# Lightning attention and a gated MLP on one core: all casts on POOL, weights requested behind them, states ahead of scores

## The chip, the cores and the metric

The kernel runs on one core of one Trainium2 chip. Its time is the device time of one execution in microseconds, the median of several runs. Five engines run their own instruction streams and wait for one another through semaphores: PE (matmul), DVE (vector), ACT (activation), POOL (GpSimd) and SP, which here only issues DMAs. ACT and POOL issue DMAs too.

## What is computed

A linear attention with decay works in blocks of 64 tokens with a running state for each head; its output, laid out as tokens by 512 channels, goes through an MLP whose gate mixes tokens. Cut to what matters:

```python
batch, n_heads, seq, head_dim = (4, 8, 768, 64)       # d_model 512, d_ff 1024
for b in range(nb):                                    # blocks of 64 tokens
    intra = einsum('bhic,bhjc->bhij', qb, kb) * Dmask  # lam ** (i - j), i >= j
    intra = einsum('bhij,bhjd->bhid', intra, vb)
    inter = einsum('bhid,bhde->bhie', qb * lam_pow, kv_state)
    out[:, :, sl] = intra + inter
    kv_state = lam_block * kv_state + einsum('bhsd,bhse->bhde', kb * rev_pow, vb)

x = out.transpose(0, 2, 1, 3).reshape(B, S, H * D)
h = maximum(x @ w_in, 0)
u, v = h[..., :512], h[..., 512:]
v_n = (v - mean(v)) / sqrt(var(v) + 1e-6)              # over channels
v_s = einsum('ts,bsd->btd', w_spatial, v_n) + b_spatial[None, :, None]
return (u * v_s) @ w_out
```

Inputs and output are float32; the kernel works in bfloat16 with sums in float32.

## The kernel before

The kernel takes blocks of 128 tokens instead of 64, which is the same recurrence. A *step* is 256 tokens of one batch with all heads: three steps a batch, twelve in all. For each step n there are these groups, whose short names are used from here on:

- lk:n, `load_step`, five DMAs from SP: k in two halves, q, v in two halves, 1.5 MB together, into four buffers each (`fin`);
- c:n, `cast_step`: kd (k times decay), qc and vc, the bfloat16 copies. kd is DVE's in the first three steps and POOL's behind them; qc is ACT's, vc POOL's;
- T:n, `trans_step`: 16 transposes of kd and qc on PE, evicted by ACT (kT) and DVE (qT);
- A:n, `scores_step`: 16 matmuls, masked by DVE (a);
- K:n, `kv_step`: the state's update, PE and then DVE (sd, s);
- O:n, `out_step`: the states of this step and the one before times q, and a times v; ACT evicts it as xT.

For each batch b the MLP follows: pv:b:r (the half of W_in that is normalised, one for each step r; ACT's relu, then DVE's statistics, ACT's root, DVE's normalised rows vn), pu:b:r (the other half, evicted as uT), pvs:b:f (four groups of products with w_spatial and the bias, multiplied by u on DVE into gT) and po:b:r (w_out, evicted by ACT, written by an output DMA from SP). wt:s are the transposes of w_spatial, done once in three pieces and evicted by ACT as wt_sb; pvs needs all three.

Weights come through POOL's DMA queue, which casts them to bfloat16: win:1 (the half for pv, 512 KB in the core), win:0 (the half for pu), wsp (w_spatial, 1152 KB, with the bias), wout (512 KB).

The orders of PE and POOL are written out by hand (`manual_schedule`); those of DVE, ACT and SP are made by a scheduler. On PE a loop over steps puts A:n+1, O:n, K:n+1 and T:n+2, and fills in pieces of the MLP from a list `pend`. On POOL win:1 is requested first, win:0 behind the cast of step 0, wsp and wout behind that of step 1.

Of the kernel before, what the change touches and what calls it, by code (L numbers as in the profile page):

```python
# [18 lines left out]
def kernel(  # L19
# [12 lines left out]
    nc = tc.nc  # L32
    P = 128
    B, H, S, D = q.shape
    DM = H * D
    DFF = moe_w_in.shape[1]
    DH = DFF // 2
    NBLK = S // P
    NG = H // 2
    NCH = DM // P  # L40
# [16 lines left out]
        return psum.tile(shape, dt, tag="ps", name=name)  # L57


    lam_bc = const.tile([P, H], FP32)  # L60
    nc.scalar.dma_start(out=lam_bc, in_=lam.unsqueeze(0).to_broadcast((P, H)))

    st = {}

    def load_step(n):
        b, r = divmod(n, NR)
        toks = slice(r * T2, (r + 1) * T2)
        q_in = fin.tile([P, H, 2, D], FP32, tag="q_in", name=f"q_in_{n}")
        k_in = fin.tile([P, H, 2, D], FP32, tag="k_in", name=f"k_in_{n}")
        v_in = fin.tile([P, H, 2, D], FP32, tag="v_in", name=f"v_in_{n}")  # L70
# [22 lines left out]

    qpos = iota_f([P, 2, 2, D], [[1, 2], [0, 2], [2, D]], 1, 0, "qpos")

    rel = iota_f([P, 2, D], [[1, 2], [2, D]], 0, -1, "rel")

    win_sb = wpool.tile([P, NCH, DFF], BF16)
    wout_sb = wpool.tile([P, NCH, DM], BF16)
    bsp_bc = wpool.tile([P, S], BF16)  # L100
    wt_sb = wpool.tile([P, NBLK, S], BF16)
    wsp_raw = wpool.tile([P, NBLK, S], BF16)

    def load_win(f0, f1):
        nc.gpsimd.dma_start(out=win_sb[:, :, f0:f1],
                            in_=moe_w_in.rearrange("(g p) f -> p g f", p=P)[:, :, f0:f1])

    load_win(DH, DFF)
    for n in range(1, 4):
        load_step(n)  # L110


    loglam = const.tile([P, H], FP32)
    nc.scalar.activation(out=loglam, in_=lam_bc, func=AF.Ln)
# [15 lines left out]
    nc.vector.tensor_scalar(out=causal, in0=rel.rearrange("p m d -> p (m d)"), scalar1=0.0,  # L130
                            scalar2=None, op0=ALU.is_ge)
    amask = const.tile([P, 2, 2, 2, P], FP32)
    for h in range(H):
        nc.vector.tensor_scalar(out=amask[:, h // 4, h % 2, (h // 2) % 2, :], in0=causal,
                                scalar1=lm128[:, h:h + 1], scalar2=None, op0=ALU.mult)
    eps_t = const.tile([P, 1], FP32)
    nc.vector.memset(eps_t, 1e-6)
    oo128 = const.tile([P, P], BF16)
    nc.vector.memset(oo128, 1.0 / P)


    xT = {}

    def cast_step(n):
        s = st[n]
        kd = att.tile([P, 2, H, D], BF16, tag="kd", name=f"kd_{n}")
        qc = att.tile([P, 2, H, D], BF16, tag="qc", name=f"qc_{n}")
        vc = att.tile([P, H, 2, D], BF16, tag="vc", name=f"vc_{n}")
        eng = nc.vector if n < NR else nc.gpsimd
        eng.tensor_tensor(out=kd.rearrange("p c h d -> p h c d"), in0=s["k_in"],  # L150
                          in1=ldec.unsqueeze(2).unsqueeze(3).broadcast_to((P, H, 2, D)),
                          op=ALU.mult)
        nc.scalar.activation(out=qc.rearrange("p m h d -> p h m d"), in_=s["q_in"], func=AF.Copy)  # L153
        nc.gpsimd.tensor_copy(out=vc, in_=s["v_in"])  # L154
        s["kd"], s["qc"], s["vc"] = kd, qc, vc

# [112 lines left out]
    def pv(b, r):  # L269
        if r == 0:  # L270
            gmlp_tiles(b)
        x, m = xT[b], gm[b]
        vh, mv, rstd = m["vh"], m["mv"], m["rstd"]
        ps = two_banks([P, 2, DH], f"pv_{b}_{r}")
        for j in range(2):
            for c in range(NCH):
                nc.tensor.matmul(out=ps[:, j], lhsT=x[:, r, c, j * P:(j + 1) * P],  # L277
                                 rhs=win_sb[:, c, DH:DFF], start=(c == 0), stop=(c == NCH - 1))
        pair = slice(2 * r, 2 * r + 2)
        nc.scalar.activation(out=vh[:, pair, :], in_=ps, func=AF.Relu)  # L280
        for t in (2 * r, 2 * r + 1):
# [54 lines left out]
        nc.scalar.activation(out=wt_sb[:, s:s + 2, :], in_=ps[:, :, 0:S], func=AF.Copy)  # L336


    pend = []

    def fill(n):
        for _ in range(min(n, len(pend))):
            pend.pop(0)()

    def after_out(n):
        b, r = divmod(n, NR)
        pend.append(lambda: pv(b, r))
        if r == 0:
            pend.append(lambda: pu(b, 0))
        if r == NR - 1:  # L350
            pend.append(lambda: pu(b, 1))
            pend.append(lambda: pu(b, 2))
            if b == 0:
                pend.extend([lambda s=s: wt_piece(s) for s in (0, 2, 4)])
            pend.extend([lambda f=f: pvs(b, f) for f in range(NCH)])
            pend.extend([lambda i=i: po(b, i) for i in range(NR)])

    with tc.manual_schedule(engines={PE, mybir.EngineType.Pool}):
        cast_step(0)
        load_win(0, DH)  # L360
        cast_step(1)
        nc.gpsimd.dma_start(out=wsp_raw, in_=moe_w_spatial.rearrange("(a p) s -> p a s", p=P))
        nc.gpsimd.dma_start(out=bsp_bc, in_=moe_b_spatial.unsqueeze(0).to_broadcast((P, S)))
        nc.gpsimd.dma_start(out=wout_sb, in_=moe_w_out.rearrange("(t p) f -> p t f", p=P))
        trans_step(0)
        scores_step(0)
        kv_step(0)
        trans_step(1)
        load_step(4)
        fills = {0: 1, 1: 2, 2: 5}  # L370
        for n in range(NS):
            if n + 2 < NS:
                cast_step(n + 2)
            if n + 5 < NS:
                load_step(n + 5)
            if n + 1 < NS:
                scores_step(n + 1)
            out_step(n)
            after_out(n)
            if n + 1 < NS:  # L380
                kv_step(n + 1)
            f = fills.get(n, 4 + (n % 3 == 0))
            fill(f // 2)
            if n + 2 < NS:
                trans_step(n + 2)
            fill(f - f // 2)
        fill(len(pend))


# [28 lines left out]
```

## Time and profile before

| | us |
|---|---|
| median of 3 runs | 187.28 (186.24 to 187.67) |
| the profiled execution | 188.46 |
| its span | 186.7 |
| PE busy in it | 145.7 (78%) |
| DVE, ACT, POOL busy | 103.4, 89.1, 34.8 |
| HBM read, written | 24.78 MB, 6.29 MB |

A profile row with a start says: start, duration, engine, line, operation, output and inputs, shapes, count, and in brackets how long the engine idled before and what ended that. Rows of grouped instructions give the total, then the mean of one in ns. A windows row gives a stretch, its length, and the busy time of each engine with its number of instructions; then the granted PE clock (1.00 is full), the share of the DMA engines and what they moved in GB/s. PE's busy time is partly modelled. Times within the span are what the text reckons with; the time of an execution is 1.76 us longer than its span here.

### The profile page before, as it was taken

Reading aid. Unit: us, or ns where it says so; the run is one execution under the profiler, and the core shown is the slowest. Engines: PE = TensorE matmul, PEld = TensorE weight load, DVE = VectorE, ACT = ScalarE, POOL = GpSimd, SP = SyncE. Lnnn points to the kernel's source line nnn. Section 1 sums busy time; section 2 is a strip of 40 time slices with the busy share of each in tenths; the row PEclk is TensorE's granted clock in tenths of the full one; section 3 lists DMA queues with packets and bytes.
Section 4 is the critical chain, followed back from the end, with each engine's and each line's share of the span. In section 5 each row is a group of like instructions: output and inputs, shape, how many; then the busy total and the mean of one; then the engine's idle time right before and its main releaser. Section 6 shows DMA issues by size and latency. Waiting matters only on the chain.

```text
span 186.7 us, 3638 instructions
## 1 busy us (share of the span) xinstructions
PE 145.7 (78%) x1540; PEld 96.5 (52%) x1540; DVE 103.4 (55%) x191; ACT 89.1 (48%) x98; POOL 34.8 (19%) x35
## 2 busy tenths in 40 slices
PE   0005677507979779999997999999799999999980
PEld 0005563305649556655776665575676646565430
DVE  1029993705399853542989747169884722564400
ACT  4244324712677942268775613666722157660051
POOL 4004060006245344060606005020000000000000
PEclk9999996975999979999999999999999999999999
DMA  4999969999999999999998900530000027000035
GB/s 98 218 211 252 205 161 184 199 212 232 199 241 248 200 239 238 221 225 222 330 254 195 252 8 0 208 133 4 0 0 4 2 79 262 0 0 4 0 132 205
DMA packets 68337, 28.36 MB, mean 152 GB/s; under 512 B 50528, under 2 KB 65248, under 8 KB 68320
## 3 DMA queue, kind: packets, MB, share of 16 engines
q1 hardware_dynamic: 65664, 25.17, 56.5%
q0 software_dynamic: 2512, 2.95, 9.6%
q8 instruction: 12, 0.20, 0.5%
q14 instruction: 5, 0.04, 0.1%
q10 hardware_dynamic: 144, 0.00, 0.0%
HBM read 24.78 MB, written 6.29 MB: 166 GB/s over the span
## 4 chain that ended last, share of the span: by engine, by line
PE 54%; SPq 13%; DVE 11%; ACT 9%; DMA 9%; issue 2%; POOL 1%; ACTq 0%; POOLq 0%
PE pvs L307 17%; PE po L322 11%; DMA v_in<-in_v_dram 9%; PE pv L277 8%; PE pu L297 7%; SPq L77 6%; SPq L72 5%; PE pt L163 4%; DVE a L192 3%; PE pvs L309 3%; SPq L74 3%; DVE st L282 3%; ACT vh L280 2%; ACT wt_sb L336 2%; DVE vn L288 2%
## 5 line engine op out<-in xcount | busy, mean ns | idle before, releaser
L307 PE MATMUL pvs<-wt_sb,vn 128*128 128x384 bf16 x192 | 37.8, 331 | 2.1 <-ACT wt_sb L336 2.0
L192 DVE TENSOR_TENSOR a<-pam,amask 128x1024 bf16<-128x1024 f32 x24 | 28.5, 1210 | 6.0 <-PE pam L189 6.0
L154 POOL CAST vc<-v_in 128x1024 bf16<-128x1024 f32 x12 | 12.9, 1074 | 84.0 <-DMA v_in<-in_v_dram 42.7
L252 ACT ACTIVATE xT<-pat 128x1024 bf16<-128x1024 f32 x12 | 15.8, 1320 | 23.7 <-PE pat L249 23.6
L307 PEld LDWEIGHTS <-vn 128*128 128x128 bf16 x192 | 18.9, 99 | 14.9 <-issue 2.5
L297 PE MATMUL pu<-xT,win_sb 128*128 128x256 bf16 x192 | 24.4, 285 | 1.9 <-DVE a L192 1.9
L311 DVE TENSOR_TENSOR gT<-pvs,uT 128x768 bf16<-128x768 f32 x16 | 15.3, 958 | 18.2 <-PE pvs L309 18.1
L277 PE MATMUL pv<-win_sb,xT 128*128 128x512 bf16 x96 | 24.2, 400 | 1.2 <-ACT xT L252 1.2
L322 PE MATMUL po<-wout_sb,gT 128*128 128x512 bf16 x96 | 21.9, 379 | 1.5 <-DVE a L192 1.1
L297 PEld LDWEIGHTS <-win_sb 128*128 128x128 bf16 x192 | 19.2, 102 | 5.7 <-issue 1.8
L153 ACT ACTIVATE qc<-q_in 128x1024 bf16<-128x1024 f32 x12 | 12.7, 1055 | 19.0 <-DMA q_in<-in_q_dram 19.0
L325 ACT ACTIVATE o<-po 128x1024 f32<-128x1024 f32 x12 | 12.3, 1025 | 19.0 <-PE po L322 19.0
L282 DVE BATCH_NORM_STATS2 st<-vh 128x6 f32<-128x512 bf16 x24 | 15.6, 682 | 10.4 <-ACT vh L280 10.3
L163 PE MATMUL pt<-ident,kd 128*128 128x128 bf16 x96 | 8.6, 242 | 15.5 <-DVE kd L150 15.5
L170 DVE TENSOR_TENSOR qT<-pt,lq 128x1024 bf16<-128x1024 bf16 x12 | 8.2, 684 | 18.5 <-ACT kT L168 18.5
L150 POOL TENSOR_TENSOR kd<-k_in,ldec 128x1024 bf16<-128x1024 f32 x9 | 17.1, 1897 | 6.1 <-DMA k_in<-in_k_dram 6.1
L168 ACT ACTIVATE kT<-pt 128x1024 bf16<-128x1024 bf16 x12 | 12.2, 1021 | 11.2 <-PE pt L163 11.2
L280 ACT ACTIVATE vh<-pv 128x1024 bf16<-128x1024 f32 x12 | 12.3, 1024 | 8.8 <-PE pv L277 8.8
L163 PEld LDWEIGHTS <-kd 128*128 128x128 bf16 x96 | 7.2, 110 | 17.4 <-DVE kd L150 15.7
L277 PEld LDWEIGHTS <-xT 128*128 128x128 bf16 x96 | 9.5, 102 | 11.7 <-issue 1.7
L322 PEld LDWEIGHTS <-gT 128*128 128x128 bf16 x96 | 9.2, 98 | 11.9 <-issue 1.0
L299 ACT ACTIVATE uT<-pu 128x1024 bf16<-128x1024 f32 x12 | 12.2, 1020 | 5.9 <-PE pu L297 5.8
(52 smaller groups left out, 146.2 us busy)
## 6 DMA issues: line engine op xcount, KB each, us to landing
k_in<-in_k_dram SPq DMA_DIRECT2D x24, 256.0 KB, 5.8
q_in<-in_q_dram SPq DMA_DIRECT2D x12, 512.0 KB, 6.1
v_in<-in_v_dram SPq DMA_DIRECT2D x24, 256.0 KB, 6.0
out_dram<-o SPq DMA_DIRECT2D x12, 512.0 KB, 3.4
wsp_raw<-in_moe_w_spatial_dram POOLq DMA_DIRECT2D x1, 1152.0 KB, 11.3
win_sb<-in_moe_w_in_dram POOLq DMA_DIRECT2D x2, 512.0 KB, 8.4
wout_sb<-in_moe_w_out_dram POOLq DMA_DIRECT2D x1, 512.0 KB, 14.8
bsp_bc<-in_moe_b_spatial_dram POOLq DMA_DIRECT2D x1, 192.0 KB, 11.7
```

The costliest lines, as they stand in the source:

```text
L150: eng.tensor_tensor(out=kd.rearrange("p c h d -> p h c d"), in0=s["k_in"], in1=ldec.unsqueeze(2).unsqueeze(3).broadcast_to((P, H, 2, D)), ...
L154: nc.gpsimd.tensor_copy(out=vc, in_=s["v_in"])
L163: nc.tensor.transpose(out=pt[:, j, g, c * P:(c + 1) * P], in_=src[:, c, 2 * g:2 * g + 2, :].rearrange("p h d -> p (h d)"), identity=ident)
L192: nc.vector.tensor_tensor(out=a_sb[:, i].rearrange("p h g c x -> p (h g) c x"), in0=pam.rearrange("p h g c x -> p (h g) c x"), in1=amask[: ...
L252: nc.scalar.activation(out=xT[b][:, r].rearrange("p g (c d m) -> p (g c) m d", c=2, m=2), in_=po.rearrange("p g c (m d) -> p (g c) m d", m ...
L277: nc.tensor.matmul(out=ps[:, j], lhsT=x[:, r, c, j * P:(j + 1) * P], rhs=win_sb[:, c, DH:DFF], start=(c == 0), stop=(c == NCH - 1))
L280: nc.scalar.activation(out=vh[:, pair, :], in_=ps, func=AF.Relu)
L282: nc.vector.bn_stats(out=m["st6"][:, t, :], in_=vh[:, t, :])
L297: nc.tensor.matmul(out=ps[:, f], lhsT=win_sb[:, c, f * P:(f + 1) * P], rhs=x[:, r, c, :], start=(c == 0), stop=(c == NCH - 1))
L307: nc.tensor.matmul(out=ps[:, i, 0:HW_], lhsT=m["vn"][:, s, f * P:(f + 1) * P], rhs=wt_sb[:, s, cols], start=(s == 0), stop=False)
L311: nc.vector.tensor_tensor(out=m["gT"][:, f, :].rearrange("p (i x) -> p i x", i=2), in0=ps[:, :, 0:HW_], in1=m["uT"][:, f, :].rearrange("p ...
L322: nc.tensor.matmul(out=ps[:, j], lhsT=gT[:, c, t * P:(t + 1) * P], rhs=wout_sb[:, c, :], start=(c == 0), stop=(c == NCH - 1))
```

## The change

All twelve casts of q and k join those of v on POOL, with four buffers each instead of three. The weights are requested behind casts: win:1 behind that of step 0, win:0, wsp and wout behind that of step 2. In the first steps K comes ahead of A. T, A, K and O of step 3 come behind the first two pvs of batch 0; before, T and A of steps 3 and 4 stood ahead of them. SP's order is now written by hand too, and the constants are formed a little earlier. Everything up to step 5 is a list of words, the rest a loop with a rule for each position in a batch.

```diff
+    ctx.enter_context(tc.manual_schedule(engines={PE, mybir.EngineType.Pool,
+                                                  mybir.EngineType.SP}))
+    for n in range(4):
+        load_step(n)
...
-    load_win(DH, DFF)
-    for n in range(1, 4):
-        load_step(n)
...
+    sq_t = const.tile([P, 1], FP32)
+    nc.scalar.activation(out=sq_t, in_=eps_t, func=AF.Sqrt)
...
+    def load_wsp():
+        nc.gpsimd.dma_start(out=wsp_raw, in_=moe_w_spatial.rearrange("(a p) s -> p a s", p=P))
+        nc.gpsimd.dma_start(out=bsp_bc, in_=moe_b_spatial.unsqueeze(0).to_broadcast((P, S)))
...
     def cast_step(n):
         s = st[n]
-        kd = att.tile([P, 2, H, D], BF16, tag="kd", name=f"kd_{n}")
...
-        eng = nc.vector if n < NR else nc.gpsimd
-        eng.tensor_tensor(out=kd.rearrange("p c h d -> p h c d"), in0=s["k_in"],
...
-        nc.scalar.activation(out=qc.rearrange("p m h d -> p h m d"), in_=s["q_in"], func=AF.Copy)
+        kd = att.tile([P, 2, H, D], BF16, tag="kd", bufs=4, name=f"kd_{n}")
...
+        nc.gpsimd.tensor_tensor(out=kd.rearrange("p c h d -> p h c d"), in0=s["k_in"],
...
+        nc.gpsimd.tensor_copy(out=qc.rearrange("p m h d -> p h m d"), in_=s["q_in"])
         nc.gpsimd.tensor_copy(out=vc, in_=s["v_in"])
...
-    with tc.manual_schedule(engines={PE, mybir.EngineType.Pool}):
-        cast_step(0)
-        load_win(0, DH)
-        cast_step(1)
...
+    run("""
+        mask c:0 win:1 c:1 c:2 win:0 wsp wout c:3 lk:4 lk:5 lk:6
+        T:0 K:0 A:0 O:0 pv:0:0 T:1 K:1 A:1 O:1 T:2 K:2 pv:0:1 A:2 pu:0:0 O:2
+        c:4 pu:0:1 pv:0:2 pu:0:2 wt:0 wt:2 wt:4
+        c:5 lk:7 pvs:0:0 pvs:0:1 T:3 pvs:0:2 A:3 K:3 c:6 pvs:0:3 T:4 po:0:0
...
+    for n in range(2 * NR - 1, NS):
...
+        if n == 2 * NR - 1:
+            run(f"pv:{b}:2 {nxt} pu:{b}:2")
...
```

POOL's queue in the front, before; vc_174, vc_181 and vc_283 are the copies of v of steps 0, 1 and 2:

```order
L105 DMA win_sb<-in_moe_w_in_dram 128x4x512
L154 CAST vc_174<-v_in_86 128x1024
L105 DMA win_sb<-in_moe_w_in_dram 128x4x512
L154 CAST vc_181<-v_in_117 128x1024
L362 DMA wsp_raw<-in_moe_w_spatial_dram 128x6x768
L363 DMA bsp_bc<-in_moe_b_spatial_dram 128x768
L364 DMA wout_sb<-in_moe_w_out_dram 128x4x512
L154 CAST vc_283<-v_in_125 128x1024
```

The same place now; steps 0, 1 and 2 are vc_173, vc_180 and vc_186, each behind its kd and qc:

```order
L164 CAST vc_173<-v_in_91 128x1024
L142 DMA win_sb<-in_moe_w_in_dram 128x4x512
L160 TENSOR_TENSOR kd_178<-k_in_95,ldec 128x8x2x64
L163 CAST qc_179<-q_in_94 128x8x2x64
L164 CAST vc_180<-v_in_99 128x1024
L160 TENSOR_TENSOR kd_184<-k_in_103,ldec 128x8x2x64
L163 CAST qc_185<-q_in_102 128x8x2x64
L164 CAST vc_186<-v_in_107 128x1024
L142 DMA win_sb<-in_moe_w_in_dram 128x4x512
L146 DMA wsp_raw<-in_moe_w_spatial_dram 128x6x768
L147 DMA bsp_bc<-in_moe_b_spatial_dram 128x768
L150 DMA wout_sb<-in_moe_w_out_dram 128x4x512
```

Each request for weights has moved behind a cast: one half of W_in from ahead of vc of step 0 to behind it, the other with wsp and wout to behind vc of step 2.

ACT ahead of the first pvs, before; pu_2 is pu:0:2, wt_sb the three pieces of w_spatial, qc_747 a cast of a later step, xT_781 the eviction of O:3:

```order
L299 ACTIVATE uT_390<-pu_2_700 128x4x256
L336 ACTIVATE wt_sb<-pwt_718 128x1536
L336 ACTIVATE wt_sb<-pwt_732 128x1536
L153 ACTIVATE qc_747<-q_in_287 128x8x2x64
L252 ACTIVATE xT_781<-pat_782 128x8x2x64
L336 ACTIVATE wt_sb<-pwt_832 128x1536
```

The same place now; kT_730 is the eviction of T:3:

```order
L310 ACTIVATE uT_317<-pu_2_607 128x4x256
L295 ACTIVATE rstd_321<-mv_320,eps_t 128x2
L347 ACTIVATE wt_sb<-pwt_625 128x1536
L347 ACTIVATE wt_sb<-pwt_639 128x1536
L347 ACTIVATE wt_sb<-pwt_653 128x1536
L178 ACTIVATE kT_730<-pt_713 128x1024
```

The cast is gone from ACT, and the attention of step 3, from its transposes to its output, has moved from ahead of the last piece of w_spatial to behind all three.

More of the change, by code (lines that the diff above doesn't have):

```diff
@@ L142, with load_wout @@
+    def load_wout():
+        nc.gpsimd.dma_start(out=wout_sb, in_=moe_w_out.rearrange("(t p) f -> p t f", p=P))
     xT = {}
@@ L358 @@
-    with tc.manual_schedule(engines={PE, mybir.EngineType.Pool}):
-        cast_step(0)
-        load_win(0, DH)
-        cast_step(1)
[L362 to L387, printed above, removed]
+    acts = {"c": cast_step, "T": trans_step, "A": scores_step, "K": kv_step, "O": out_step,
+            "lk": load_step, "pv": pv, "pu": pu, "pvs": pvs,
+            "po": po, "wt": wt_piece, "win": load_win, "wsp": load_wsp, "wout": load_wout,
+            "mask": make_amask}
@@ L391 @@
+    run(" ".join([f"pvs:{B - 1}:{f}" for f in range(NCH)] + [f"po:{B - 1}:{r}" for r in range(NR)]))
 _INS = ['q', 'k', 'v', 'lam', 'moe_w_in', 'moe_w_spatial', 'moe_b_spatial', 'moe_w_out']
```

122 lines of the change are left out of this document (67 added, 55 removed).

## The prediction

> **What bounds the kernel now.** I read the windows first, cut at three places that the chain of waits names: the first states of step 2 (43.09), the first spatial product that runs through (66.49), the last matmul (182.57). After the times stand PE, PEld, DVE, ACT and POOL busy, the granted clock, the DMA share and GB/s.
>
> ```profile
> span 186.7 us, 3638 instructions
> ...
> 0.00:43.09 43.09, 14.68 (x192) 10.67 (x193) 20.62 (x40) 16.32 (x21) 8.53 (x17) 0.92 0.97 192
> 43.09:66.49 23.40, 19.54 (x265) 15.05 (x265) 18.47 (x32) 16.96 (x17) 10.44 (x7) 0.92 1.14 232
> 66.49:182.57 116.08, 111.46 (x1084) 70.80 (x1083) 64.36 (x120) 55.77 (x60) 15.81 (x12) 0.99 0.46 120
> 182.57:186.70 4.13, 0.00 (x0) 0.00 (x0) 0.00 (x0) 0.01 (x1) 0.00 (x0) 1.00 0.48 180
> ```
>
> From 66.49 to 182.57 PE works 111.46 of 116.08 us: it is the bound there, and only 4.6 us can be had. Ahead of 66.49 it works 14.68 + 19.54 = 34.2 us, so 32.3 us are idle. The front is where time can be won. The chain of waits in order of time says what it waits for:
>
> ```profile
> 25.91 15.96 DMA v_in<-in_v_dram
> ...
> 42.00 1.05 POOL vc L154
> 43.09 0.43 PE pkv L207 x6
> ...
> 65.14 1.30 ACT wt_sb L336
> 66.49 0.48 PE pvs L307 x2
> ```
>
> The last load of step 2 takes 16 us. What else is under way is on POOL, whose timeline holds the casts and its own requests for weights; the page's DMA issues add how long the weights take to land (last number):
>
> ```profile
> 1.81 0.95 POOL L105 DMA_DIRECT2D win_sb<-in_moe_w_in_dram  x1
> 13.71 1.46 POOL L154 CAST vc<-v_in 128x1024 bf16<-128x1024 f32 x1 [10.94 <-DMA v_in<-in_v_dram]
> 15.12 0.76 POOL L105 DMA_DIRECT2D win_sb<-in_moe_w_in_dram  x1
> 24.46 1.04 POOL L154 CAST vc<-v_in 128x1024 bf16<-128x1024 f32 x1 [8.58 <-DMA v_in<-in_v_dram]
> 25.44 0.83 POOL L362 DMA_DIRECT2D wsp_raw<-in_moe_w_spatial_dram  x1
> 26.81 0.76 POOL L364 DMA_DIRECT2D wout_sb<-in_moe_w_out_dram  x1
> 43.81 1.90 POOL L150 TENSOR_TENSOR kd<-k_in,ldec 128x1024 bf16<-128x1024 f32 x1 [0.77 <-DMA k_in<-in_k_dram]
> 64.85 1.90 POOL L150 TENSOR_TENSOR kd<-k_in,ldec 128x1024 bf16<-128x1024 f32 x1 [0.78 <-DMA k_in<-in_k_dram]
> ```
>
> ```profile
> wsp_raw<-in_moe_w_spatial_dram POOLq DMA_DIRECT2D x1, 1152.0 KB, 11.3
> win_sb<-in_moe_w_in_dram POOLq DMA_DIRECT2D x2, 512.0 KB, 8.4
> wout_sb<-in_moe_w_out_dram POOLq DMA_DIRECT2D x1, 512.0 KB, 14.8
> ```
>
> All weights were asked for by 26.81 and had landed by 41.6 (26.8 + 14.8), just when the last piece of step 2 came: they had passed it on the DMA engines. Without weights a step lands every 7.0 us (k of step 3 cast at 43.81, of step 6 at 64.85; 21.04 / 3).
>
> **The change part by part.**
>
> *Weights behind the casts.* How much transfer a half of W_in is: wout, the same size and last in its queue, came 41.6 - 36.7 = 4.9 us after wsp (25.4 + 11.3), with v of step 2 beside it; alone it lies between 2 and 4.9, and I take 2.8. In the old order v of step 1 landed at 24.46 behind both halves. Now only win:1 goes before it, so 24.46 - 2.8 = 21.7, and step 2 comes one step later, 28.7 at the latest. Some bytes of step 2 had already moved by 24.46, so I take 28.0, and 29.0 for the end of vc of step 2 (bounds 26 and 30). Before it was 43.05: 14.0 us earlier.
>
> *What step 2 no longer waits for, others do.* win:0, wsp and wout are requested only at 29.0. In PE's order pu:0:0, which needs win:0, stands ahead of O:2, so the queue stops there until 29.0 + 8.4 = 37.4. Ahead of that, win:1 is requested behind vc of step 0 (13.71 + 1.46 - 2.8 = 12.4), lands by 12.4 + 8.4 = 20.8, and pv:0:0 waits for it with T:1 behind. Prices for what follows:
>
> ```profile
> 43.45 3.54 PE L297 MATMUL pu<-xT,win_sb 128*128 128x256 bf16 x16
> 52.95 1.90 PE L277 MATMUL pv<-win_sb,xT 128*128 128x512 bf16 x8 [1.16 <-ACT xT L252]
> 54.69 1.91 PE L297 MATMUL pu<-xT,win_sb 128*128 128x256 bf16 x16
> 56.44 0.61 PE L163 MATMUL pt<-ident,kd 128*128 128x128 bf16 x8
> 60.82 0.62 PE L189 MATMUL pam<-qT,kT 64*128 64x128 bf16 x16 [0.24 <-DVE qT L170]
> 61.70 0.41 PE L242 MATMUL pat<-qT,s 64*64 64x128 bf16 x8 [0.26 <-ACT wt_sb L336]
> 62.04 0.64 PE L249 MATMUL pat<-a,vc 128*64 128x128 bf16 x16
> 62.54 0.44 PE L207 MATMUL pkv<-vc,kd 128*64 128x64 bf16 x16
> 63.04 0.83 PE L333 MATMUL pwt<-ident,wsp_raw 128*128 128x128 bf16 x12
> ```
>
> ```profile
> L336 ACT ACTIVATE wt_sb<-pwt 128x1536 bf16<-128x1536 bf16 x3 | 4.3, 1459 | 0.0
> ```
>
> Between 20.8 and 37.4 PE has pv 1.9 twice, T 0.9 twice, K 0.4 twice, A 0.6 twice and O:1 1.0: 8.6 us, which leaves 8 for the DVE and ACT steps between them; so the wait for win:1 is hidden by that for win:0. From 37.4 on: pu:0:0 1.9, O:2 about 1.0 (0.41 + 0.64), pu:0:1 1.9 (it covers ACT's xT of O:2), pv:0:2 1.9, pu:0:2 1.9, the first transposes of w_spatial 0.8, then three evictions on ACT, 4.4: together 13.8, so 51.2. The other way in: wsp, second in its queue, lands some 15 us after the request (8.4 for win:0, then 1152 KB at wout's rate, between 4.5 and 11, taken at 6.5), 44, and with 0.8 + 4.4 that gives 49.2. The later one decides: the full run of spatial products begins at 51.2 instead of 66.49, -15.3.
>
> *Work that the earlier start leaves behind.* By 66.49 the old order had done T, A and K of steps 3 and 4 and O:3; the new one does them behind the first products, where PE is the bound. T is two groups like the pt row, one for kd and one for qc, which overlap by a quarter (0.9); A 0.6, K 0.4, O:3 about 0.9: 2 x 1.9 + 0.9 = 4.7, less overlaps 4.4. So +4.4.
>
> *States ahead of scores.* K now stands ahead of A in steps 0 to 2, so DVE's copy of the state waits for vc and qT stands behind it; in the front this waits for the same v that O needs anyway, and is hidden behind the wait for win:1 and win:0: nothing. Behind it K costs 0.4 wherever it stands.
>
> *All casts on POOL.* ACT gives up twelve qc, DVE three kd; both had room. POOL gains them:
>
> ```profile
> L153 ACT ACTIVATE qc<-q_in 128x1024 bf16<-128x1024 f32 x12 | 12.7, 1055 | 19.0 <-DMA q_in<-in_q_dram 19.0
> L150 POOL TENSOR_TENSOR kd<-k_in,ldec 128x1024 bf16<-128x1024 f32 x9 | 17.1, 1897 | 6.1 <-DMA k_in<-in_k_dram 6.1
> ```
>
> qc on POOL is not in the trace; it lies between vc (1.04) and kd, whose output is permuted too (1.90). I take 1.1, since like vc it has one input. A step then costs POOL 4.0 of the 7.0 us between loads: POOL doesn't fall behind. Its longer occupation of something DVE needs is another matter:
>
> ```profile
> 63.98 0.42 DVE L218 TENSOR_TENSOR sd<-s,l 128x256 f32<-128x256 bf16 x1
> 64.89 2.14 DVE L218 TENSOR_TENSOR sd<-s,l 128x256 f32<-128x256 bf16 x1
> ```
>
> The same sd takes 0.42 alone and 2.14 when it starts beside the kd of 64.85, and ends just behind it. So DVE can be held for what POOL gains: 12 x 1.1 + 3 x 1.9 = 19 us (12 x 1.9 + 5.7 = 28.5 at most), if every POOL cast met such an operation on PE's path. DVE is busy 64.36 of 116.08 us, and in the old order such meetings cost PE little of its 4.6 idle us; I take +0.5 (bounds 0 and 19).
>
> The Trainium skill (SBUF — State Buffer, Who interferes with whom) says that DVE and GpSimd share a port pair which one of them holds for a whole instruction while the other fully blocks, for DVE operations with two SBUF inputs as well as its fast modes. The two rows agree; by that rule taken to its end the sum would be 19 us more.
>
> *The later stages.* One place has less cover: between pv:1:2 and pvs:1:0, which needs its normalised rows, there were two pu beside A, O and K, and now there are a T and one pu. The old order's only wait there is
>
> ```profile
> 100.31 1.91 PE L297 MATMUL pu<-xT,win_sb 128*128 128x256 bf16 x16 [0.94 <-DVE a L192]
> ```
>
> and 1.9 - 0.9 = 1.0 of cover is gone: +1.0 (bounds 0 and 2). The loads hide behind PE: k of step 8, the tightest, came at 64.85 + 2 x 7.0 = 78.9 and q within the next half of its 7.0 us, 82; batch 0's outputs (1.5 MB, 7 us at most, as much as a step) now go ahead of it on SP's queue: 89, and 3.0 for kd and qc: 92. PE needs them some 42 us of matmuls behind 51.2, at 93. That a buffer is freed by POOL alone costs nothing: it is filled again four steps later.
>
> *Sum.* -15.3 + 4.4 + 0.5 + 1.0 = -9.4. The profiled execution took 188.46 us, of which 1.76 lie outside its span: 186.7 - 9.4 = 177.3 for the span and 179.1 for it. The median of the runs is 187.28, 1.2 below it, so **177.9 us** is forecast against that.
>
> **The rivals.**
>
> *PE runs its front at half the clock.* After 8 us of idling pu took 3.54 us (43.45) against 1.91 (54.69). The granted clock stood at 0.50 then:
>
> ```profile
> 44.00:46.00 2.00, 2.00 (x12) 1.38 (x11) 1.96 (x3) 0.30 (x1) 1.71 (x1) 0.50 1.29 291
> ```
>
> The new order has PE wait up to 5 us for win:0, then again near 44. If only pu:0:0 is slow, +1.6; if all 9.4 us of matmuls from pu:0:0 to the transposes are, +9.4 (187.3). Against it: the work behind the wait is dense, and the old order was at full clock again by 48. Its typical price is +6: 184. The Trainium skill (TensorE: Matmul & The Clock Gate, The HAM clock gate) has the clock halve after an idle window of about 3.4 us and return after as much sustained work. By that rule the price would be 3.4 / 2 = 1.7 us a wait, an estimate from the page; the 4 us at half rate after 43.09 agree in kind.
>
> *The loads become the bound.* If an output costs its full 7 us and the first stages run well, T:8 waits: the slack worked out above is 1 us, so a wait of up to 5 us gives 178 to 183. For it: the share of DMA is 1.14 from 43.09 to 66.49, so the transfers have no room. Against: the old order's loads let PE idle for only 4.6 us from 66.49 on.
>
> *The gain is larger.* If step 2 ends at 26 and win:0 lands in 6 us, the products begin near 46; the loads of step 8 then stop PE, so no more than 5 us come of it: 173.
>
> *Slower: POOL holds DVE.* One mechanism, at each sd and vn on the way from pv to pvs and from pkv to pat. It decides from 9.4 + 1.9 = 11.3 us on PE's path, more than half of the 19 worked out; at 15 the time is 192. For it: sd at 64.89. Against it: DVE's 45% of idle time, and that in the old order 4.6 us is all that PE lost to anything.
>
> *It doesn't do what it says.* If v of step 2 is late for a reason of its own on SP's queue, the weights come later still; the front is then as long as before plus the 4.4 left behind and minus nothing: 187 to 192. Against it stands that the steps without weights beside them land every 7.0 us.
>
> **How the numbers follow.** Forecast (174 to 182.5) 0.60; half clock 0.11; loads as bound 0.10; larger gain 0.08; POOL holding DVE 0.06; front not shortened 0.05. The range leaves out the two last and the tails: 171.5 to 184.5. A measurement tells about 1% from no change, 185.4 and 189.2 here. Below 185.4 lie the forecast, the loads, the larger gain and most of the half clock: 0.88. Within lie the rest of the half clock and some of the last: 0.05. Above: 0.07.
>
> **What would show it.** Right: vc of step 2 ends near 29 with the requests for win:0 and wsp behind it; PE waits at pu:0:0 for a DMA until about 37; the third wt_sb ends near 51; from there PE is busy 116 of some 122 us. Wrong: win:0 landing after 41 or vc of step 2 after 32 (front), a granted clock at 0.50 for over 6 us behind 37, sd and vn groups with a mean over 1 us and PE waiting for them (POOL), or T:8 waiting for q_in or k_in (loads).

## The result, and the profile after

| | before | changed |
|---|---|---|
| median, us | 187.47 (186.24 to 189.24, 4 runs) | 180.58 (178.63 to 185.14, 4 runs) |
| ratio | | 0.962, 95% interval 0.950 to 0.974 |
| the profiled execution, its span | 188.46, 186.7 | 178.63, 176.8 |
| DVE, ACT, POOL busy | 103.4, 89.1, 34.8 | 102.6, 78.8, 53.1 |

The change makes the kernel 3.8% faster; the medians differ by 6.89 us. Ratios leave out executions that lie over 1.5% above the fastest of their kernel (the profiled ones of e4, e5 and e10 below are such), while medians hold all. The two profiled executions lie 9.83 us apart and the medians 6.89, so the spans below overstate the gain.

The windows of the changed kernel, cut at the end of the cast of v of step 2, at the third wait for wt_sb and behind the last matmul. The columns are those of the windows before.

```profile
span 176.8 us, 3630 instructions
...
0.00:28.97 28.97, 12.56 (x151) 8.97 (x153) 15.44 (x33) 12.20 (x18) 14.15 (x20) 0.96 0.99 201
28.97:52.05 23.08, 18.22 (x186) 12.67 (x184) 11.23 (x22) 13.28 (x13) 8.89 (x9) 0.83 1.14 217
52.05:172.70 120.65, 114.13 (x1195) 73.75 (x1203) 75.98 (x133) 53.26 (x57) 30.01 (x23) 1.00 0.56 139
172.70:176.80 4.10, 0.00 (x0) 0.00 (x0) 0.00 (x0) 0.03 (x1) 0.00 (x0) 1.00 0.49 183
```

The products begin at 52.05 instead of 66.49: 14.44 us earlier. The stretch behind them takes 120.65 instead of 116.08 us: 4.57 longer. The weight loads show why (fourth column of the stretch): 1203 instead of 1083, and 120 is exactly what T, A and K of steps 3 and 4 and O:3 hold (32 for each of T, A and K over the two steps, 24 for O:3). Some matmul records are missing here (1195 beside 1203 loads). The balance is 14.44 - 4.57 = 9.87 us, the span's 186.7 - 176.8 = 9.9.

POOL's timeline of the changed kernel answers to the casts and requests shown of before; two rows of its DMA issues follow, with the time to landing last.

```profile
27.93 1.04 POOL L164 CAST vc<-v_in 128x1024 bf16<-128x1024 f32 x1 [1.02 <-DMA v_in<-in_v_dram]
28.91 0.83 POOL L142 DMA_DIRECT2D win_sb<-in_moe_w_in_dram  x1
29.74 0.83 POOL L146 DMA_DIRECT2D wsp_raw<-in_moe_w_spatial_dram  x1
```

```profile
wsp_raw<-in_moe_w_spatial_dram POOLq DMA_DIRECT2D x1, 1152.0 KB, 14.0
win_sb<-in_moe_w_in_dram POOLq DMA_DIRECT2D x2, 512.0 KB, 8.0
```

The v of step 2 is cast by 28.97 (before: 43.05). The chain of waits in order of time tells what then sets the front:

```profile
19.82 0.59 PE pv L287
...
20.63 2.76 PE pv L287 x6
23.41 1.03 ACT vh L290
24.47 1.29 DVE st L293 x2
...
27.27 1.14 DVE a L202
...
29.44 1.14 DVE a L202
30.62 0.64 PE pat L259 x8
31.26 1.82 PE pt L173 x16
...
34.20 2.77 PE pv L287 x6
...
37.34 1.23 DVE a L202
...
46.77 1.02 ACT uT L310
...
47.98 4.03 ACT wt_sb L347 x3
```

From 19.8 on no transfer stands in it. PE, ACT and DVE pass the work to one another. PE runs pv:0:0 and pv:0:1 at half their rate (2.76 us for six matmuls, where eight take 1.90 at full rate), and A:1, a and O:1 stand behind DVE's statistics of the first pv. The granted clock explains the second of the two only. Two windows, one in each:

```profile
20.00:22.00 2.00, 1.78 (x5) 0.70 (x5) 0.00 (x0) 0.00 (x0) 1.04 (x1) 1.00 0.82 133
34.00:36.00 2.00, 1.80 (x5) 0.70 (x5) 0.69 (x1) 0.14 (x1) 0.81 (x1) 0.50 1.19 198
```

At pv:0:1 it stands at 0.50; at pv:0:0, as slow, at 1.00. Why pv:0:0 is slow stays open.

The third wait for wt_sb, with which the products begin, and the three long waits of PE behind it:

```profile
52.05 0.48 PE L318 MATMUL pvs<-wt_sb,vn 128*128 128x384 bf16 x2 [0.85 <-ACT wt_sb L347]
...
66.33 0.62 PE L199 MATMUL pam<-qT,kT 64*128 64x128 bf16 x16 [0.82 <-DVE qT L180]
...
85.66 1.90 PE L287 MATMUL pv<-win_sb,xT 128*128 128x512 bf16 x7 [1.17 <-ACT xT L262]
...
94.25 0.66 PE L318 MATMUL pvs<-wt_sb,vn 128*128 128x384 bf16 x2 [1.06 <-DVE vn L299]
```

The groups on POOL, and DVE's sd, the state times its decay (total, mean of one in ns):

```profile
L160 POOL TENSOR_TENSOR kd<-k_in,ldec 128x1024 bf16<-128x1024 f32 x12 | 22.9, 1910 | 26.4 <-DMA k_in<-in_k_dram 22.2
...
L163 POOL CAST qc<-q_in 128x1024 bf16<-128x1024 f32 x12 | 13.0, 1083 | 2.4 <-DMA q_in<-in_q_dram 2.4
L228 DVE TENSOR_TENSOR sd<-s,l 128x256 f32<-128x256 bf16 x16 | 12.8, 800 | 0.4
```

A qc takes POOL 1.08 us, what it took ACT (1.06). The mean of sd has risen from 573 to 800 ns; in the runs below that have the same casts on POOL it lies between 589 (e1) and 800.

### The profile page after: what moved, and what is told of

Its sections match the earlier page's. It is cut to its first block, busy times and chain, and to the rows that moved or that the text cites. A ratio compares the mean times of both kernels' runs of the same rounds, so it can differ in the third digit from the quotient of the medians.

```text
span 176.8 us, 3630 instructions
## 1 busy us (share of the span) xinstructions
PE 144.9 (82%) x1528; PEld 95.4 (54%) x1540; DVE 102.6 (58%) x187; ACT 78.8 (45%) x88; POOL 53.1 (30%) x50
## 4 chain that ended last, share of the span: by engine, by line
PE 64%; DVE 18%; ACT 7%; DMA 3%; SPq 2%; issue 2%; POOL 1%; ACTq 0%; POOLq 0%
PE pvs L318 16%; PE pv L287 13%; PE po L333 11%; PE pu L308 10%; DVE a L202 8%; PE pt L173 4%; DMA v_in<-in_v_dram 3%; PE pat L259 3%; PE pvs L320 3%; ACT wt_sb L347 2%; DVE gT L322 2%; DVE st L293 2%; DVE sd L228 2%; PE pam L199 2%; DVE qT L180 2%
## 5 line engine op out<-in xcount | busy, mean ns | idle before, releaser
L318 PE MATMUL pvs<-wt_sb,vn 128*128 128x384 bf16 x192 | 37.1, 326 | 3.5 <-ACT wt_sb L347 2.3
L160 POOL TENSOR_TENSOR kd<-k_in,ldec 128x1024 bf16<-128x1024 f32 x12 | 22.9, 1910 | 26.4 <-DMA k_in<-in_k_dram 22.2
L287 PE MATMUL pv<-win_sb,xT 128*128 128x512 bf16 x89 | 25.2, 418 | 3.3 <-ACT xT L262 2.6
L322 DVE TENSOR_TENSOR gT<-pvs,uT 128x768 bf16<-128x768 f32 x16 | 15.3, 956 | 18.4 <-PE pvs L320 18.4
L308 PE MATMUL pu<-xT,win_sb 128*128 128x256 bf16 x192 | 22.5, 273 | 0.0
L308 PEld LDWEIGHTS <-win_sb 128*128 128x128 bf16 x192 | 18.5, 98 | 3.1
L163 POOL CAST qc<-q_in 128x1024 bf16<-128x1024 f32 x12 | 13.0, 1083 | 2.4 <-DMA q_in<-in_q_dram 2.4
L228 DVE TENSOR_TENSOR sd<-s,l 128x256 f32<-128x256 bf16 x16 | 12.8, 800 | 0.4
```

The source lines that it names most:

```text
L160: nc.gpsimd.tensor_tensor(out=kd.rearrange("p c h d -> p h c d"), in0=s["k_in"], in1=ldec.unsqueeze(2).unsqueeze(3).broadcast_to((P, H, 2, ...
L163: nc.gpsimd.tensor_copy(out=qc.rearrange("p m h d -> p h m d"), in_=s["q_in"])
L228: nc.vector.tensor_tensor(out=sd, in0=prev, in1=lb, op=ALU.mult)
L308: nc.tensor.matmul(out=ps[:, f], lhsT=win_sb[:, c, f * P:(f + 1) * P], rhs=x[:, r, c, :], start=(c == 0), stop=(c == NCH - 1))
L318: nc.tensor.matmul(out=ps[:, i, 0:HW_], lhsT=m["vn"][:, s, f * P:(f + 1) * P], rhs=wt_sb[:, s, cols], start=(s == 0), stop=False)
L322: nc.vector.tensor_tensor(out=m["gT"][:, f, :].rearrange("p (i x) -> p i x", i=2), in0=ps[:, :, 0:HW_], in1=m["uT"][:, f, :].rearrange("p ...
```

## The experiments

The time came out near the forecast. What had to be settled was whether it came for the reasons given, since one sign of the forecast is missing: PE reaches pu:0:0 at 37.45, as forecast, but directly behind A:2 and not out of a wait for win:0. All runs are listed here; "products begin" is the third wait for wt_sb in the profiled execution.

| kernel | median, us | ratio to before (95%) | products begin | from there to the span's end |
|---|---|---|---|---|
| before | | | 66.49 | 120.2 |
| changed | 180.58 | 0.962 (0.950 to 0.974) | 52.05 | 124.8 |
| e1 weights early | 184.35 | 0.988 (0.974 to 1.002) | 55.53 | 126.5 |
| e2 weights late only | 187.84 | 1.015 (1.008 to 1.022) | 68.31 | 118.5 |
| e3 casts as before | 188.34 | 1.017 (1.011 to 1.024) | 59.95 | 126.8 |
| e4 scores first | 185.10 | 0.991 (0.984 to 0.998) | 52.65 | 130.1 |
| r1 changed, again | 180.54 | 0.961 (0.952 to 0.969) | 51.80 | 124.2 |
| e5 pv behind scores | 177.93 | 0.952 (0.945 to 0.960) | 50.59 | 128.7 |
| e6 old group order | 183.76 | 0.987 (0.980 to 0.993) | 60.40 | 121.8 |
| e7 more cover | 177.75 | 0.953 (0.946 to 0.960) | 52.86 | 123.1 |
| e8 front and cover | 174.05 | 0.936 (0.929 to 0.943) | 47.63 | 124.8 |
| e9 only qc on ACT | 186.46 | 1.008 (1.003 to 1.013) | 57.52 | 127.0 |
| e10 only kd on DVE | 179.20 | 0.964 (0.957 to 0.971) | 50.70 | 129.2 |
| e11 qc on ACT from step 6 | 183.84 | 0.990 (0.985 to 0.995) | 51.55 | 130.0 |

The last column of e4, e5 and e10 is not compared.

**Which part brings it: weights or casts.** e1 is the changed kernel with the weights requested as early as before.

```diff
-        mask c:0 win:1 c:1 c:2 win:0 wsp wout c:3 lk:4 lk:5 lk:6
+        mask win:1 c:0 win:0 c:1 wsp wout c:2 c:3 lk:4 lk:5 lk:6
```

> The changed kernel with the weights requested as they were: win:1 first of all, win:0 behind the casts of step 0, wsp and wout behind those of step 1. Theory (the weights passed step 2's v on the DMA engines): vc of step 2 ends near 43 again instead of 29, the full run of spatial products begins near 61 instead of 52, the span is 185 to 187 and the time 187 to 189, so the whole gain is gone though order and casts are the new ones. Rival (the order of the groups and the casts on POOL bring the gain): the span stays within 2 us of 176.8.

The v of step 2 came late, though its cast ended at 36.74 and not near 43, and K:2 waited for it. POOL's and then PE's timeline:

```profile
35.70 1.04 POOL L164 CAST vc<-v_in 128x1024 bf16<-128x1024 f32 x1 [6.25 <-DMA v_in<-in_v_dram]
```

```profile
36.79 0.43 PE L217 MATMUL pkv<-vc,kd 128*64 128x64 bf16 x8 [1.28 <-POOL vc L164]
```

But PE waited 1.28 us for it and not 8, and the products began at 55.53, only 3.5 us behind the changed kernel's 52.05. So 11 of the 14.4 us are there with the weights where they were. The theory was right in direction and wrong in size. The kernel loses more than the front does, 0.988 beside 0.962: from 90 to 100 us PE idles 3.87 us in e1 and 1.51 in the changed kernel, most of it ahead of pvs:1:0 for vn, which is taken up again below.

e2 goes the other way: the kernel before, with nothing changed but the requests (win:1 behind the cast of step 0, the others behind that of step 2).

```diff
-    load_win(DH, DFF)
...
-        load_win(0, DH)
+        load_win(DH, DFF)
...
+            if n == 0:
+                load_win(0, DH)
...
```

> The kernel before with one edit: win:1 is requested behind vc of step 0, win:0, wsp and wout behind vc of step 2; casts and orders stay. Theory: vc of step 2 ends near 29, but PE's old order has T, A and K of steps 3 and 4 ahead of the last piece of w_spatial, and those loads now run beside the weights; the products begin near 60 and the span is 180 to 182, about half of the gain. Rival (the weights alone are the whole gain): span 176 to 178. Second rival (step 2's v is late for another reason): vc of step 2 still ends beyond 38.

The cast of v of step 2 ends at 27.50, near the 29 that was expected, and yet the kernel gains nothing: it is 1.5% slower. ACT's and PE's timelines of e2 show what the earlier v ran into:

```profile
50.36 1.06 ACT L152 ACTIVATE qc<-q_in 128x1024 bf16<-128x1024 f32 x1 [6.28 <-DMA q_in<-in_q_dram]
51.33 1.28 ACT L251 ACTIVATE xT<-pat 128x1024 bf16<-128x1024 f32 x1
```

```profile
52.66 3.59 PE L276 MATMUL pv<-win_sb,xT 128*128 128x512 bf16 x8 [7.02 <-ACT xT L251]
```

In ACT's order a qc of a later step stands ahead of xT. Its q has not landed, ACT stands idle for 6.28 us, and PE loses 7.02 us to an eviction that had nothing to do with that load. The kernel before has such a wait on ACT too, nearly as long as PE's wait for v (8.07 us, until 43.09):

```profile
45.70 1.06 ACT L153 ACTIVATE qc<-q_in 128x1024 bf16<-128x1024 f32 x1 [7.72 <-DMA q_in<-in_q_dram]
```

So the two limits lie close together there, and in e2 lifting one of them uncovered the other.

e3 takes the changed kernel and moves the casts back: kd of steps 0 to 2 to DVE, all qc to ACT.

```diff
-        nc.gpsimd.tensor_tensor(out=kd.rearrange("p c h d -> p h c d"), in0=s["k_in"],
+        eng = nc.vector if n < NR else nc.gpsimd
+        eng.tensor_tensor(out=kd.rearrange("p c h d -> p h c d"), in0=s["k_in"],
...
-        nc.gpsimd.tensor_copy(out=qc.rearrange("p m h d -> p h m d"), in_=s["q_in"])
+        nc.scalar.activation(out=qc.rearrange("p m h d -> p h m d"), in_=s["q_in"], func=AF.Copy)
```

> The changed kernel with kd of steps 0 to 2 on DVE and all qc on ACT, as they were. Theory (casts on POOL neither cost nor bring anything by themselves): span within 1 us of 176.8. Rival (POOL's casts hold DVE on PE's path): 2 us or more faster, with the mean of sd back from 800 ns towards 573 ns and the products beginning ahead of 50. Second rival (the casts on POOL are part of the gain): 2 us or more slower.

The whole gain is gone, though the weights come as late as in the changed kernel. Which of the two casts does it, and how, was the question of three later runs, each the changed kernel with one edit. e9 has only the qc on ACT:

```diff
-        nc.gpsimd.tensor_copy(out=qc.rearrange("p m h d -> p h m d"), in_=s["q_in"])
+        nc.scalar.activation(out=qc.rearrange("p m h d -> p h m d"), in_=s["q_in"], func=AF.Copy)
```

> The changed kernel, with the twelve qc on ACT again, kd all on POOL. In ACT's order the qc of step 4 stands ahead of vh of pv:0:2, uT of pu:0:2 and the three wt_sb. Theory (a cast that waits for a late load holds up ACT's evictions behind it): q_in of step 4 lands near 51, ACT idles 5 to 6 us there, products begin at 58 to 60 instead of 52, time 185 to 188. Rival (DVE's kd were what cost in the kernel with all casts moved back): products begin near 52 and the time is 179 to 182.

e10 has only kd of steps 0 to 2 on DVE:

```diff
-        nc.gpsimd.tensor_tensor(out=kd.rearrange("p c h d -> p h c d"), in0=s["k_in"],
+        eng = nc.vector if n < NR else nc.gpsimd
+        eng.tensor_tensor(out=kd.rearrange("p c h d -> p h c d"), in0=s["k_in"],
```

> The changed kernel, with kd of steps 0 to 2 on DVE again and qc all on POOL. Theory (late loads in ACT's queue are what counts): k of steps 0 to 2 lands before DVE gets there or within 1 us, so nothing is lost in the front: products begin at 51 to 53, time 178 to 182. Rival (DVE's kd, 1.9 us each among the copies of the scores, are what cost in the kernel with all casts moved back): products begin at 56 or later and the time is 184 to 188.

e10 is as fast as the changed kernel (0.964 beside 0.962), with the products at 50.70. e9 loses everything (1.008). ACT's timeline of e9, then PE's:

```profile
43.84 1.02 ACT L310 ACTIVATE uT<-pu 128x1024 bf16<-128x1024 f32 x1 [0.54 <-PE pu L308]
50.38 1.06 ACT L163 ACTIVATE qc<-q_in 128x1024 bf16<-128x1024 f32 x1 [5.53 <-DMA q_in<-in_q_dram]
51.35 1.01 ACT L290 ACTIVATE vh<-pv 128x1024 bf16<-128x1024 f32 x1
52.25 1.02 ACT L310 ACTIVATE uT<-pu 128x1024 bf16<-128x1024 f32 x1
53.16 1.45 ACT L347 ACTIVATE wt_sb<-pwt 128x1536 bf16<-128x1536 bf16 x1
```

```profile
45.36 1.91 PE L308 MATMUL pu<-xT,win_sb 128*128 128x256 bf16 x16
47.11 1.50 PE L344 MATMUL pwt<-ident,wsp_raw 128*128 128x128 bf16 x24
52.40 0.83 PE L344 MATMUL pwt<-ident,wsp_raw 128*128 128x128 bf16 x12 [3.79 <-ACT vh L290]
...
57.52 0.80 PE L318 MATMUL pvs<-wt_sb,vn 128*128 128x384 bf16 x2 [0.54 <-ACT wt_sb L347]
```

PE had finished pv:0:2, pu:0:2 and two of the three transposes of w_spatial by 48.6. ACT could have evicted all of them, but its next instruction was the qc of step 4, whose q landed at 50.4. The evictions behind it start 5.5 us late, the products 57.52 - 52.05 = 5.5 us late.

e11 asked whether it is this wait or merely ACT's time that counts: qc of steps 0 to 5 on POOL, of steps 6 to 11 on ACT.

```diff
+        if n < 6:
+            nc.gpsimd.tensor_copy(out=qc.rearrange("p m h d -> p h m d"), in_=s["q_in"])
+        else:
+            nc.scalar.activation(out=qc.rearrange("p m h d -> p h m d"), in_=s["q_in"], func=AF.Copy)
```

> The changed kernel, with qc of steps 6 to 11 on ACT, the first six on POOL. ACT carries half of what it carried before, but from step 6 on the loads come 7 us apart and ahead of need. Theory (not the 1.06 us of a cast but its wait for a load counts): products begin near 52 as in the changed kernel, ACT's qc wait only while ACT has nothing else to do, and POOL is free sooner: time 177.5 to 181. Rival (ACT has no room for the casts): half of the loss of the kernel with all casts moved back, 183 to 185.

The front came out as expected (51.55), the time did not: 183.84, the rival's number. The trace does not show the rival's reason, though. ACT's timeline, then PE's:

```profile
64.32 1.06 ACT L166 ACTIVATE qc<-q_in 128x1024 bf16<-128x1024 f32 x1 [6.69 <-DMA q_in<-in_q_dram]
```

```profile
67.06 0.62 PE L202 MATMUL pam<-qT,kT 64*128 64x128 bf16 x16 [2.06 <-DVE qT L183]
...
86.60 0.63 PE L255 MATMUL pat<-qT,s 64*64 64x128 bf16 x16 [1.39 <-ACT vh L293]
...
89.67 1.90 PE L290 MATMUL pv<-win_sb,xT 128*128 128x512 bf16 x8 [1.62 <-ACT xT L265]
```

ACT was idle for 6.69 us ahead of the qc, so it had room; it was the order again, with kT, vh and xT behind casts whose loads were not there. What was wrong is my belief that the loads from step 6 on come ahead of ACT's need: the scheduler had put each cast too early in ACT's order. Two of these waits stand in the changed kernel as well, but shorter (0.82 and 1.17 us). Over the whole stretch behind 51.55 PE idles 11.0 us (125.85 - 114.83), where the changed kernel in its second run, r1, idles 5.5 (120.07 - 114.61): the difference is that of their spans, 181.5 and 176.0.

**What sets the front now.** e4 and e5 test whether it is the chain of PE, DVE and ACT. e4 puts the scores ahead of the states again in steps 0 to 2:

```diff
-        T:0 K:0 A:0 O:0 pv:0:0 T:1 K:1 A:1 O:1 T:2 K:2 pv:0:1 A:2 pu:0:0 O:2
+        T:0 A:0 K:0 O:0 pv:0:0 T:1 A:1 K:1 O:1 T:2 A:2 pv:0:1 K:2 pu:0:0 O:2
```

> The changed kernel with A ahead of K in steps 0 to 2. Theory: the place of K is hidden behind other waits of the front; span within 1 us of 176.8 and the products begin within 1 us of 52. Rival (states ahead of scores is a part of the gain): 1.5 us or more slower.

The products begin at 52.65 instead of 52.05, a difference that tells nothing by itself. But the whole kernel is 3% slower than the changed one by the ratios, with intervals apart (0.984 to 0.998 and 0.950 to 0.974): the rival came true, and the theory did not. In the profile the loss is behind the front. From 90 to 100 us PE idles 4.40 us, again most of it for vn, where the changed kernel idles 1.51, and the granted clock falls to 0.83 from 50 to 60 and from 100 to 110. It is one execution, and one that the ratio leaves out, so the cause stays open.

e5 keeps K first, but lets T and A of step 1 go ahead of pv:0:0, and A:2 ahead of pv:0:1, so that DVE's scores no longer queue behind the statistics; pu:0:0 goes behind O:2, and pv:0:2 and pu:0:1 change places, which the expectation doesn't say:

```diff
-        T:0 K:0 A:0 O:0 pv:0:0 T:1 K:1 A:1 O:1 T:2 K:2 pv:0:1 A:2 pu:0:0 O:2
-        c:4 pu:0:1 pv:0:2 pu:0:2 wt:0 wt:2 wt:4
+        T:0 K:0 A:0 O:0 T:1 K:1 A:1 pv:0:0 O:1 T:2 K:2 A:2 pv:0:1 O:2
+        pu:0:0 c:4 pv:0:2 pu:0:1 pu:0:2 wt:0 wt:2 wt:4
```

> The changed kernel with the front of PE's order rearranged: T:1 directly behind O:0, pv:0:0 between A:1 and O:1, pv:0:1 between A:2 and O:2, pu:0:0 behind O:2. Nothing else moves. Theory (the front of the changed kernel is a chain of PE, DVE and ACT steps in which pv stands ahead of the next T, and not a wait for win:0): the products begin at 49 to 50.5 instead of 52, bounded by w_spatial's landing near 43.7; 1.5 to 3 us faster than the changed kernel. Rival (the wait for win:0 at 37 sets the front, as predicted): the products begin within 0.5 us of 52.

The products begin at 50.59, and here the wait that I had forecast appears on PE:

```profile
36.64 3.03 PE L308 MATMUL pu<-xT,win_sb 128*128 128x256 bf16 x16 [0.44 <-DMA win_sb<-in_moe_w_in_dram]
```

In the changed kernel win:0 lands near 36.9 (28.91 + 8.0, an estimate) and the chain reaches pu:0:0 at 37.45. So the two limits lie within a microsecond of each other.

**Behind the front.** e6 restores the order in which T, A and K of steps 3 and 4 and O:3 stand ahead of the last piece of w_spatial:

```diff
-        c:4 pu:0:1 pv:0:2 pu:0:2 wt:0 wt:2 wt:4
-        c:5 lk:7 pvs:0:0 pvs:0:1 T:3 pvs:0:2 A:3 K:3 c:6 pvs:0:3 T:4 po:0:0
-        A:4 O:3 K:4 po:0:1 c:7 po:0:2 lk:8 T:5 pv:1:0
+        c:4 pu:0:1 pv:0:2 T:3 pu:0:2 wt:0 A:3 K:3 T:4 wt:2 A:4 O:3 K:4 wt:4
+        c:5 lk:7 pvs:0:0 pvs:0:1 pvs:0:2 c:6 pvs:0:3 po:0:0
+        po:0:1 c:7 po:0:2 lk:8 T:5 pv:1:0
```

> The changed kernel with T, A, K of steps 3 and 4 and O:3 ahead of the last piece of w_spatial again, as in the kernel before; casts and weights as changed. Theory (these groups wait for step 4, which lands near 54 since the weights run beside it): the products begin at 57 to 60, the work behind them is 4.4 us less, and the time is 1 to 4 us above the changed kernel. Rival (the place of these groups is worth nothing): within 1 us of it.

The products begin at 60.40, the stretch behind is 3 us shorter (121.8 beside 124.8), and the kernel is slower than the changed one: 0.987, its interval above the changed kernel's. PE waits at T:4 for POOL's kd, whose k lands only at 50.0:

```profile
51.97 1.03 PE L173 MATMUL pt<-ident,kd 128*128 128x128 bf16 x8 [3.62 <-POOL kd L160]
```

e7 gives the statistics of batch 1 more cover: pu:1:0 and pu:1:1 move from ahead of pv:1:1 and behind it to either side of pv:1:2.

```diff
-        A:5 O:4 K:5 pu:1:0 lk:9 T:6 pv:1:1 pu:1:1
+        A:5 O:4 K:5 lk:9 T:6 pv:1:1
...
-            run(f"pv:{b}:2 {nxt} pu:{b}:2")
+            run(f"pu:{b}:0 pv:{b}:2 {nxt} pu:{b}:1 pu:{b}:2")
```

> The changed kernel with two pu groups of batch 1 moved: pu:1:0 to between K:6 and pv:1:2, where PE waits for ACT's xT, and pu:1:1 to between T:7 and pu:1:2, ahead of pvs:1:0. Theory (PE loses 1.2 us to xT and 1 to 4 us at pvs:1:0, the latter by the luck of a POOL cast beside vn): 1.5 to 3 us faster than the changed kernel in the median, no wait for vn above 0.5 us. Rival (PE is the bound there and the waits come back elsewhere): within 0.7 us of it.

PE's waits for xT at pv:1:2 and for vn at pvs:1:0 (1.17 and 1.06 in the changed kernel) are gone; 0.90 us for a stand ahead of pvs:1:0 instead. r1 is the changed kernel once more, without an edit, on the same chip:

> The changed kernel itself, beside the three below on one chip, and a second look at what differs between its executions. Theory: the front repeats (products begin at 51 to 53), and what varies is the start of pvs:1:0, which waits for vn while POOL's kd of step 8 or 9 holds DVE: span 176.8 where vn of the last rows of batch 1 takes 1.1 us, 179 to 182 where it takes 2.4 to 3.1. Rival (the front varies): the beginning of the products moves by more than 2 us.

The front repeats (51.80), and PE waits 0.69 us for vn. e5 and e7 are each about 1% below r1, though with intervals that overlap r1's. e8 has both edits, the diffs of e5 and e7 together:

> The changed kernel with both earlier edits: scores ahead of pv in the front (alone about 1.5 us better than the changed kernel), and pu:1:0 and pu:1:1 kept back as cover for the statistics of batch 1 (alone also about 1.5 us better). If the front is a chain of waits and the place before pvs:1:0 another, they are separate and add up: products begin near 50.6, no wait of PE over 1 us behind that, span near 174, time 175 to 176.5. Rival: an earlier front only lets PE meet the loads or POOL's kd elsewhere, so the second edit adds nothing: 177.5 to 178, with a new wait of 1 to 2 us behind 52.

It is the fastest, 0.936 (0.929 to 0.943), below the changed kernel's interval. Its windows, cut at its third wait for wt_sb, and PE's row of pu:0:0:

```profile
0.00:47.63 47.63, 28.99 (x336) 20.69 (x337) 27.84 (x54) 25.29 (x31) 20.89 (x26) 1.00 1.11 212
47.63:168.25 120.62, 114.74 (x1204) 74.01 (x1203) 75.73 (x133) 53.33 (x57) 31.85 (x24) 1.00 0.59 145
```

```profile
35.35 1.92 PE L308 MATMUL pu<-xT,win_sb 128*128 128x256 bf16 x16 [0.22 <-DMA win_sb<-in_moe_w_in_dram]
```

The products begin 3.0 us earlier than in the profile of e5, which has the same front. Of that, 1.3 us are win:0, which lands earlier (pu:0:0 starts at 35.35 and not at 36.64), and 1.7 are the rate of PE: pu:0:0 and pv:0:2 took 1.92 and 1.89 us here, 3.03 and 2.50 in e5. The mean granted clock was 0.971 to 0.997 in e8's six executions and 0.963 to 0.980 in r1's, so a part of e8's gain may be the clock; how much was not measured. The stretch behind is as long as in the changed kernel's profile (120.62 and 120.65), so the cover's worth rests on e7's ratio and not on this profile.

## Why the prediction came out as it did

The forecast was 177.9 us and the measured median 180.58, inside the range, and faster as forecast. The gain was forecast as 9.4 us; the medians give 6.89, the ratio 3.8%. The spans of the two profiled executions give 9.9, nearer to the sum than the medians, but that is partly luck, since these two lie further apart than the medians do. By its steps:

*The products begin at 51.2.* Measured 52.05, so -14.4 where the sum had -15.3. The forecast was a walk through the new order from a few anchors, and most anchors held: vc of step 2 at 29.0 (28.97), win_sb 8.4 to landing (8.0), the last wt_sb at 51.2 (52.0).

*What carried it: the step that failed.* The prediction put the whole of it under "Weights behind the casts". e1 shows 3.5 us of it for the weights; 11 us are there without them. And it priced the step "All casts on POOL" at nothing ("both had room"). e9 shows that taking the qc off ACT is worth 5.5 us of the front and, by the ratios, the whole gain (1.008 instead of 0.962); e10 shows that the kd on DVE are worth nothing that these runs can tell, as long as the qc are on POOL. I had counted what a cast costs the engine (1.06 us) and not what stands behind it while it waits for its load (5 to 7 us in e2, e3 and e9). The row for it was in the prediction: the group of qc had 19.0 us of idle time in front of it, all for q_in. I read that as idle time on an engine with room. It came out near the truth because the walk went through ACT's new order, in which no cast stands among the evictions: the walk had the benefit in it without knowing where it came from. That is luck too. The wait stands at the very start of the kernel before as well: ldec, which kd of step 0 needs, is formed on ACT at 12.73, behind a qc that waited 6.06 us for its q, and T:0 begins at 14.33; in the changed kernel it begins at 8.11.

*No part does it alone.* Late weights with the old casts gain nothing (e2: 1.015, e3: 1.017), since an early v only lets the next thing in ACT's queue wait. Casts on POOL with early weights gain little (e1: 0.988, with an interval that takes in 1). The old order of the groups (e6: 0.987) and scores ahead of states (e4: 0.991) each take more than half of the gain away too, so what each part takes away alone adds up to far more than the whole gain. SP's order by hand, the earlier constants and the fourth buffers were not tried alone.

*"PE stops at pu:0:0 until 37.4."* The number was met (37.45), the reason was not: a chain over DVE and ACT ended there. This sign alone would have passed for a proof; the row's bracket, with no DMA in it, said otherwise, and e5 made the wait visible by shortening the chain. In the old order the same wait is long: in e2 PE waits 5.86 us for win:0 ahead of pu:0:0.

*Work left behind, +4.4, and less cover, +1.0.* The stretch behind grew by 4.57 where the terms, with the +0.5 for POOL holding DVE, had 5.9. With all records there (r1), PE's work in that stretch is 114.61 us beside 111.46 before. That is 3.15 more, but the kernel before ran the first microseconds of its stretch at a low clock:

```profile
66.49:72.00 5.51, 5.51 (x35) 3.82 (x35) 1.59 (x3) 2.08 (x2) 1.30 (x2) 0.69 1.27 235
```

By this clock some 1.7 us of it were lost (5.51 x 0.31, an estimate), so the moved groups cost about 4.9 and the 4.4 was near. What the sum lacked is those 1.7 us, which the changed kernel doesn't pay behind its front. PE's wait at pvs:1:0 is 1.06, as forecast; the 1.17 at pv:1:2 for xT was not foreseen, and e7 shows that both go with more cover.

*States ahead of scores, nothing.* Not borne out: with scores first again the kernel loses 2.9% (e4, 0.991 beside 0.962), most of what the whole change gains. The prediction looked at the front alone, where the profiles differ by 0.6 us; the loss is behind it, and its cause is open.

*POOL holding DVE, +0.5.* A qc took 1.08 (taken 1.1). The rival did not come to its 11 us, but it is there: DVE's sixteen sd cost 12.8 us instead of 9.2 (9.4 in e1). Where it meets PE's path is the last rows of vn ahead of pvs:1:0, and what it costs there depends on when POOL's casts fall beside them. DVE's and POOL's rows of e1:

```profile
97.19 2.48 DVE L299 TENSOR_SCALAR vn<-vh,mv,rstd 128x512 bf16<-128x512 bf16 x2
```

```profile
96.58 1.90 POOL L160 TENSOR_TENSOR kd<-k_in,ldec 128x1024 bf16<-128x1024 f32 x1 [1.38 <-DMA k_in<-in_k_dram]
98.42 1.10 POOL L163 CAST qc<-q_in 128x1024 bf16<-128x1024 f32 x1
```

The same two rows of vn take 0.72 us in r1, where no kd lies beside them, and 1.09 in the changed kernel's profile; PE waits 1.73 and 0.70 us for them in e1 and 0.69 in r1. The Trainium skill (SBUF — State Buffer, Who interferes with whom) gives the rule: a DVE operation in one of the two-port modes and a GpSimd instruction shut each other out for a whole instruction. These rows agree with it for an operation with one tensor as input from SBUF; that vn runs in such a mode is not shown.

*The half-clock rival.* It did not come behind 37, where it was put, but ahead of it: 0.83 is the mean clock from 28.97 to 52.05 and 1.00 that from 37.45 on. On the chain pv:0:0 and pv:0:1 take some 1.6 us each more than at full rate, pv:0:0 while the granted clock reads 1.00. The loads (kd of a later step) did not become the bound.

## What to carry to other kernels

An instruction that waits for a load should not stand in the queue of an engine that evicts results: count for it what the engine could have done in that wait, not the microsecond that it runs. In a group row, idle time that ends with a DMA is a price once finished work stands behind it, however low the engine's busy share. When two edits each lift one of two limits that lie close together, each alone shows little. What a part is worth alone doesn't add up to the whole, and a move in the front can cost its time far behind it. And a number that is met does not prove its reason, so read the bracket of the row as well.

## What the runs showed of the hardware

The cast of q costs POOL 1.08 us and ACT 1.06, though its output is permuted; kd, with its second input, takes POOL 1.91. The time of an unchanged instruction depends on its neighbours more than I had thought: two vn rows take 0.72 us in r1 and 2.48 beside POOL in e1. Eight matmuls of pv take 1.90 or 3.59 us, and the granted clock doesn't always tell which: it reads 1.00 over the whole front of e8, whose pv:0:0 takes 3.59.
